# Where the transposing matmuls stand in a block, the place of the x loads, and how much the accumulating DMA adds

## The chip, the cores and the metric

The kernel runs on one core of one Trainium2 chip. The metric is the device time of one execution in microseconds; below it is the median of three runs. The profiled execution is a separate one, with its own time and its own span (first to last instruction).

## The reference, cut to what matters

A dynamic convolution is followed by a two-matmul block with a tanh shrink:

```
w     = softmax(weight_gen over its 7 taps)             # per token and head
conv  = sum over k of w[.., h, k] * x_pad[s + k, h, :]   # 8 heads of 24 channels
h     = conv @ w_in                                      # 192 -> 2048
out   = (h - tanh(h)) @ w_out                            # 2048 -> 192
```

There are 8 x 4096 = 32768 tokens of 192 channels.

## The kernel before, in words

**Tiling.** The tokens are cut into 32 blocks (`NTOT`) of 1024 tokens. Token p*8+j of a block lies in partition p, slot j. Taps are multiplied with the token on the partitions. The result must then be transposed, so that channels lie on the partitions for the first matmul. The 192 channels form three chunks (c = 0, 1, 2) of 64.

**Taps (`products`, L200).** For most blocks GpSimd multiplies all seven taps into three bf16 tiles: `even` (taps 0, 2, 4), `odd` (taps 1, 3, 5) and `last` (tap 6). After tap 5 an accumulating DMA on GpSimd's queue adds `odd` to `even` (L235), but only over the first `ACC` elements of a row. `ACC` is 3*8*192 - 8*64 = 4096 of 4608, so what lies beyond is chunk 2 of the third pair. Blocks 0 to 3 (`PLAIN`) don't use that DMA. The first multiplication of block n+2 is held until `gt1` of block n is done (`behind=last_sub[0]`).

**Transpose and sum (`conv_sums`, L251; `conv_out`).** TensorE multiplies each piece of 64 partitions and 128 columns by an identity, accumulating in PSUM. One chunk of one tap tile takes 8 such matmuls (4 column pieces, two partition halves). There are 4 groups (three of `even`, `last`), and chunk 2 has a fifth, `odd`'s third pair. That makes 8*(4+4+5) = 104 matmuls a block. ScalarE then copies the sums to `convT` (L292): chunk 2 as 128x512, chunks 0 and 1 together as 128x1024.

**First matmul (`gemm1`, L309).** Each of the 16 f tiles (128 of the 2048 inner features) takes 6 matmuls of 512 columns, two row halves side by side, into a PSUM tile `ph`. ScalarE writes `th` = tanh(`ph`) (L320) and VectorE writes `gt` = `ph` - `th` (L321). A `ph` tile is free for reuse only after its `gt`. `ph` and the transposes' `pc` share a rotation of three PSUM tiles (`psum_h`, `bufs=3`), so each new tile waits for the third one before it.

**Second matmul (`gemm2`, L344).** Call number i computes half of token slot i and the other half of slot i-1, alternating, in 16 steps f of two matmuls of 192 columns. There are two PSUM banks, `obank[i % 2]`. After call i, ScalarE copies slot i-1 to `out_sb` (L363). Call i+1 starts slot i+1 in that same bank, so its first matmul waits for that copy. The second matmul is one block behind the first: beside `gemm1` of block n stands `gemm2` of block n-1.

**Order.** The order is written by hand, and each engine keeps it. In block n, six or seven pairs (two `gemm1` tiles, then one `gemm2` call) come first, p = 0, 1, ... VectorE gets small softmax pieces between them: a sum at p = 1, 2, 3 (L155) and a reciprocal at p = 4, 5 (L164). The tail follows: `gemm1` 12 and 13; call 6 with the transposes of chunk 2 mixed in between its steps f = 5 to 12 and their copy after step 12; the transposes of chunks 0 and 1 in one run of 64, and their copy; two steps of call 7; the softmax's normalisation (`softmax_norm`, two VectorE instructions that use chunk 2's `pc` tile as scratch); `gemm1` 14; steps 2 to 8 of call 7; `gemm1` 15; and the rest of call 7. In blocks 1, 2 and 3 (`LATE`) the x load of block n+3 comes at the very end.

**SyncE's queue.** In a block outside `LATE` it holds the x load of block n+3 (L111), then, where a sequence begins, the six halo rows of zeros (L121), the weights of block n+4 (L97), and the output store of block n-2 (L367).

Of the kernel before, what the change touches and what calls it, by code (L numbers as in the profile page):

```python
# [16 lines left out]
def kernel(  # L17
# [10 lines left out]
    B, S, D = x.shape  # L28
    H, K = weight_gen.shape[2], weight_gen.shape[3]
# [3 lines left out]
    R = P // 2  # L33
    HALO = K - 1

    J = 8
    TOK = P * J
    JH = J // 2
    HT = TOK // 2
    NSB = S // TOK  # L40
    NTOT = B * NSB
    NFT = F // P
    NC = D // R
    GC = G // NC
    NPAIR = K // 2
    ACC = NPAIR * J * D - J * R
    PLAIN = (0, 1, 2, 3)
    assert S % TOK == 0 and D % R == 0 and H * GC == R and F % P == 0
    assert NFT == 2 * J, "one token block of the second matmul per pair of f tiles"
# [25 lines left out]
    prods_of = {}  # L75
# [27 lines left out]
    def load_x(n, behind=None):  # L103
        b, s = divmod(n, NSB)
        s0 = s * TOK

        x_t = xpool.tile([P, HALO + J, D], FP32, name="x_t")

        def rows(p0, p1, r0=0, r1=HALO + J):
            first = x[0, 0:1]  # L110
            return nc.sync.dma_start(  # L111
                out=x_t[p0:p1, r0:r1, :],
                in_=bass.AP(
                    tensor=first.tensor,
                    offset=first.offset + (b * S + s0 + p0 * J - HALO + r0) * D,
                    ap=[[J * D, p1 - p0], [D, r1 - r0], [1, D]],
                ),
            )

        def no_halo():  # L120
            nc.sync.dma_start(  # L121
                out=x_t[0:1, 0:HALO, :],
                in_=zero[:].rearrange("o (h d) -> o h d", h=1).to_broadcast([1, HALO, D]),
            )


        if n == 0:
            rows(0, P, HALO, HALO + J)
            rows(16, P, 0, HALO)
            rows(1, 16, 0, HALO)  # L130
            no_halo()
        else:
            dma = rows(0, P)
            if behind is not None:
                order(dma, behind, "order of the loads")
            if s == 0:

                no_halo()
        x_of[n] = x_t
# [11 lines left out]
    def softmax_sum(n, j0=0, j1=J):  # L151

        if j0 == 0:
            zsum_of[n] = wgpool.tile([P, J * H], FP32, name="zsum")
        nc.vector.reduce_sum(  # L155
            out=zsum_of[n][:, j0 * H : j1 * H],
            in_=e_of[n][:, j0:j1].rearrange("p j h k -> p (j h) k"),
            axis=AX.X,
        )
# [40 lines left out]
    def products(n, taps=None, sums=None, hooks={}, behind=None):  # L200

        x_t = x_of.pop(n)
        wsm, wsm_v, e_t, zr = wsm_of.pop(n)
        if e_t is not None:
            scale(nc.gpsimd, wsm[:], e_t, zr[:])
        in_pairs = n not in PLAIN

        even = ppool.tile([P, NPAIR, NC, J, H, GC], BF16, name="even")
        odd = ppool.tile([P, NPAIR, NC, J, H, GC], BF16, name="odd")
        last = ppool.tile([P, NC, J, H, GC], BF16, name="last")  # L210
        dst = {}
        for i in range(NPAIR):
            dst[2 * i] = even[:, i]
            dst[2 * i + 1] = odd[:, i]
        dst[K - 1] = last[:]
        if -1 in hooks:
            hooks[-1]()
        for eng, k, j0, j1 in taps or [(nc.gpsimd, k, 0, J) for k in range(K)]:
            w = wsm_v if eng is nc.vector else wsm[:]
            mul = eng.tensor_mul(  # L220
                dst[k][:, :, j0:j1].rearrange("p c j h g -> p j h c g"),
                x_t[:, k + j0 : k + j1, :].rearrange("p j (h c g) -> p j h c g", h=H, c=NC),
                w[:, j0:j1, :, k : k + 1]
                .rearrange("p j h (k o) -> p j h k o", o=1)
                .to_broadcast([P, j1 - j0, H, NC, GC]),
            )
            if k == 0 and behind is not None:


                order(mul, behind, "pace")  # L230
            if j1 == 1:
                first_halo[0] = mul
            if k == K - 2 and in_pairs:

                nc.gpsimd.dma_start(  # L235
                    out=even[:].rearrange("p i c j h g -> p (i c j h g)")[:, 0:ACC],
                    in_=odd[:].rearrange("p i c j h g -> p (i c j h g)")[:, 0:ACC],
                    accum_op=mybir.AluOpType.add,
                    max_dma_last_dim=4096,
                )  # L240
            if k in hooks:
                hooks[k]()
        if in_pairs:
            groups = [even[:, i] for i in range(NPAIR)] + [last[:]]
            prods_of[n] = [
                groups + ([odd[:, NPAIR - 1]] if c == NC - 1 else []) for c in range(NC)
            ]
        else:
            prods_of[n] = [[dst[k] for k in (sums or range(K))]] * NC

# [47 lines left out]
    def conv(n, *parts):  # L298
        pcs = []
        for _ in conv_sums(n, parts, pcs):  # L300
            pass
        conv_out(n, parts, pcs)

    def gemm1(n, f):
        convT = conv_of[n]
        ph = psum_h.tile([P, 2, HT], FP32, name="ph", tag="ph")
        for c in range(NC):
            for r in range(2):
                nc.tensor.matmul(  # L309
                    ph[:, r, :],  # L310
                    lhsT=w_in[r * R : (r + 1) * R, c, f * P : (f + 1) * P],
                    rhs=convT[r * R : (r + 1) * R, c, :],
                    start=(c == 0),
                    stop=(c == NC - 1),
                )
        th = tpool.tile([P, TOK], FP32, name="th")
        ph_f = ph[:].rearrange("p r t -> p (r t)")
        g1_act[0] = last_act.get(0)
        gt = gpool.tile([P, TOK], BF16, name=f"gt{f}", tag=f"gt{f}")
        last_act[0] = nc.scalar.activation(out=th[:], in_=ph_f, func=ACT.Tanh)  # L320
        last_sub[0] = nc.vector.tensor_sub(gt[:], ph_f, th[:])  # L321
        g_of.setdefault(n, []).append(gt)

    LAST = (NTOT - 1) * J
    LATE = (1, 2, 3)
    LEAD = 5
    FILL, HALF = 2, 9
    half = {}
    out_of = {}

# [139 lines left out]
    def some(sums, m):  # L470
        for _ in range(m):
            next(sums, None)

    load_wg(3)
    load_wg(4)
    for n in range(NTOT):
        if n + 3 < NTOT and n not in LATE:
            load_x(n + 3)
        for p in range(J):
            gemm1(n, 2 * p)  # L480
            gemm1(n, 2 * p + 1)
            if n == 0:


                if p == 3:
                    pcs = []
                    sums = conv_sums(1, ((0, 1),), pcs, obank)
                if 3 <= p <= 6:
                    some(sums, (3 if p == 3 else 1) * 4 * JH)
                if p == 7:  # L490
                    some(sums, K * 4 * JH)
                    conv_out(1, ((0, 1),), pcs)
                    conv(1, (2,))
                continue
            if p == 0 and n == 1:
                softmax_exp(3)
            if p == 1 and n == 1:
                softmax_norm_ramp(3)
                products(3)
            if n + 3 < NTOT:  # L500

                if p == 0:
                    softmax_exp(n + 3)
                if p == 0 and n + 4 < NTOT:
                    load_wg(n + 4)
                if 1 <= p <= 3:
                    softmax_sum(n + 3, (p - 1) * 3, min(p * 3, J))
                if 4 <= p <= 5:
                    softmax_recip(n + 3, (p - 4) * JH, (p - 3) * JH)
            if p < 6 or n == NTOT - 1:  # L510
                gemm2((n - 1) * J + p)
            if p == 0 and 1 < n < NTOT - 2:
                products(n + 2, behind=last_sub[0])
            if p == 6 and n < NTOT - 1:
                break
        if not 1 <= n < NTOT - 1:
            continue


        pcs = []  # L520
        sums = conv_sums(n + 1, ((2,),), pcs)
        mix = len(prods_of[n + 1][2]) * 2 * JH // J

        def between(f):
            if LEAD <= f:
                some(sums, mix)
            if f == LEAD + J - 1:
                conv_out(n + 1, ((2,),), pcs)

        gemm2((n - 1) * J + 6, between=between)  # L530
        conv(n + 1, (0, 1))
        gemm2((n - 1) * J + 7, 0, FILL)
        if n + 3 < NTOT:

            softmax_norm(n + 3, pcs[0][:, 0])
        gemm1(n, NFT - 2)
        gemm2((n - 1) * J + 7, FILL, HALF)
        gemm1(n, NFT - 1)
        gemm2((n - 1) * J + 7, HALF, NFT)
        if n in LATE:  # L540


            load_x(n + 3, last_conv[0])
    gemm2(LAST)
    for j in range(J):
        gemm2_last(j)
# [30 lines left out]
```

The softmax here doesn't subtract the row's maximum and nothing guards it: scores larger than these inputs give would overflow.

## Time and profile before

| | before |
|---|---|
| median of three runs | 762.88 us (762.48 to 765.41) |
| profiled execution: device time / span | 762.46 us / 760.7 us |
| TensorE granted clock | 1.0 over the whole span |
| busy: TensorE / VectorE / ScalarE / GpSimd | 97% / 89% / 84% / 88% |
| `gt`, VectorE, x512 | 603.1 us, 1220 ns each |
| `th`, ScalarE, x512 | 500.5 us, 1022 ns each |
| second matmul, x7936 | 402.6 us, 243 ns each (overlapping) |
| first matmul, x3072 | 391.3 us, 378 ns each (overlapping) |
| tap products on GpSimd, `even` and `odd` / `last` | 2.96 / 3.31 us each |
| accumulating DMA, x28 | 1205 ns of GpSimd each, 8.8 us to landing |
| copy to `convT`, 128x512 / 128x1024 | 598 / 1023 ns |
| copy to `out_sb` | 329 ns |

Busy time of matmuls overlaps, because they are pipelined and their ends are modelled, so where an instruction starts says more than how long it lasted. The middle of the run is a steady state: from the first `gemm1` of one block to that of the next it takes 22.6 us.

### The profile page before, as it was taken

To read this page: it belongs to the slowest core of one execution; us is meant where nothing else is said; L and a number is where in the kernel's file an instruction comes from. 1 tells how busy PE (TensorE), PEld (TensorE's weight loads), DVE (VectorE), ACT (ScalarE), POOL (GpSimd) and SP (SyncE) were. 2 spreads that over 40 slices of the span, in tenths; PEclk is the share of its full clock that TensorE was granted. 3 is DMA by queue.
4 is the path that set the end of the run, shared out by engine and by line. 5 is a ranking of instruction groups with operands and counts; after the bars stand their busy time and mean duration, and the time that the engine had idled before them with its cause. 6 is when DMAs were issued, how large, how long until landed. Compare 5 with 4: busy or idle time off the path is not lost.

```text
span 760.7 us, 32533 instructions
## 1 busy us (share of the span) xinstructions
PE 737.8 (97%) x14848; PEld 575.5 (76%) x14848; DVE 676.3 (89%) x737; ACT 642.3 (84%) x869; POOL 668.7 (88%) x262
## 2 busy tenths in 40 slices
PE   3799999999999999999999999999999999999997
PEld 2477777777778777777877777877777777777777
DVE  7988898989999999999999999998999999998893
ACT  4888888888888888888888888888888888888882
POOL 8999999999999999999999999999999999999000
PEclk9999999999999999999999999999999999999999
DMA  8903347576555775545775655666555577552212
GB/s 216 234 24 129 135 123 186 146 193 146 124 155 157 184 184 130 132 143 149 184 185 130 150 134 149 174 183 171 124 125 151 167 183 180 111 128 62 76 43 85
DMA packets 25399, 110.04 MB, mean 145 GB/s; under 512 B 4671, under 2 KB 9519, under 8 KB 21294
## 3 DMA queue, kind: packets, MB, share of 16 engines
q1 hardware_dynamic: 14718, 77.03, 28.5%
q0 software_dynamic: 10544, 30.94, 25.6%
q8 instruction: 116, 1.90, 1.0%
q14 instruction: 21, 0.17, 0.1%
HBM read 54.52 MB, written 25.17 MB: 105 GB/s over the span
## 4 chain that ended last, share of the span: by engine, by line
PE 93%; DVE 4%; DMA 1%; ACT 1%; issue 1%; ACTq 0%; DVEq 0%
PE obank L344 43%; PE ph L309 43%; PE pc L268 6%; DVE gt L321 3%; PE po L379 1%; DMA x_t<-in_x_dram 1%; DVE odd L220 0%; DMA wg_t<-in_weight_gen_dram 0%; DVE even L220 0%; ACT th L320 0%; DVE zsum L155 0%; ACT e_t L144 0%; DVE zr L164 0%; DVE wsm L194 0%; ACT convT L286 0%
## 5 line engine op out<-in xcount | busy, mean ns | idle before, releaser
L321 DVE TENSOR_TENSOR gt<-ph,th 128x1024 bf16<-128x1024 f32 x512 | 603.1, 1220 | 65.1 <-ACT th L320 61.3
L320 ACT ACTIVATE th<-ph 128x1024 f32<-128x1024 f32 x512 | 500.5, 1022 | 63.0 <-PE ph L309 57.9
L344 PE MATMUL obank<-w_out,gt 64*128 64x192 bf16 x7936 | 402.6, 243 | 1.9 <-issue 0.9
L309 PE MATMUL ph<-convT,w_in 64*128 64x512 bf16 x3072 | 391.3, 378 | 5.0 <-DVE gt L321 2.7
L344 PEld LDWEIGHTS <-gt 64*128 64x128 bf16 x7936 | 350.0, 94 | 59.6 <-issue 1.1
L220 POOL TENSOR_TENSOR even<-x_t,wsm 128x1536 bf16<-128x1536 f32 x93 | 275.2, 2959 | 22.6 <-DVE gt L321 22.4
L220 POOL TENSOR_TENSOR odd<-x_t,wsm 128x1536 bf16<-128x1536 f32 x93 | 275.0, 2957 | 0.0
L309 PEld LDWEIGHTS <-w_in 64*128 64x128 bf16 x3072 | 172.8, 94 | 107.2 <-issue 19.4
L220 POOL TENSOR_TENSOR last<-x_t,wsm 128x1536 bf16<-128x1536 f32 x32 | 105.9, 3308 | 0.0
L363 ACT ACTIVATE out_sb<-obank 128x192 f32<-128x192 f32 x248 | 81.7, 329 | 7.4 <-PE obank L344 3.1
L292 ACT ACTIVATE convT<-pc 128x512 bf16<-128x512 f32 (+1 forms) x63 | 50.7, 807 | 28.4 <-PE pc L268 28.4
L268 PE MATMUL pc<-ident,even 64*128 64x64 bf16 x2256 | 57.2, 191 | 1.2 <-issue 0.9
L268 PEld LDWEIGHTS <-even 64*128 64x128 bf16 x2304 | 54.2, 96 | 2.2 <-issue 1.3
L235 POOL DMA_DIRECT2D even<-odd x28 | 33.7, 1205 | 8.7 <-POOL odd L220 8.7
L268 PE MATMUL pc<-ident,last 64*128 64x64 bf16 x752 | 27.4, 191 | 9.3 <-POOL last L220 9.3
L155 DVE TENSOR_REDUCE zsum<-e_t 128x24 f32<-128x168 f32 (+2 forms) x88 | 27.5, 312 | 3.0 <-ACT e_t L144 3.0
L268 PEld LDWEIGHTS <-last 64*128 64x128 bf16 x768 | 20.2, 96 | 9.6 <-POOL last L220 9.3
L144 ACT ACTIVATE e_t<-wg_t 128x448 f32<-128x448 f32 x32 | 18.4, 578 | 7.3 <-DMA wg_t<-in_weight_gen_dram 7.3
L164 DVE RECIPROCAL zr<-zsum 128x32 f32<-128x32 f32 (+1 forms) x58 | 20.3, 350 | 0.1
L268 PE MATMUL pc<-ident,odd 64*128 64x64 bf16 x464 | 18.8, 197 | 1.7 <-POOL odd L220 0.7
L194 DVE TENSOR_TENSOR wsm<-e_t,pc 128x448 f32<-128x448 f32 x28 | 17.4, 622 | 2.9
L268 PEld LDWEIGHTS <-odd 64*128 64x128 bf16 x512 | 15.4, 99 | 2.5 <-POOL odd L220 0.9
(27 smaller groups left out, 64.3 us busy)
## 6 DMA issues: line engine op xcount, KB each, us to landing
x_t<-in_x_dram SPq DMA_DIRECT2D x31, 1344.0 KB, 9.4
even<-odd POOLq DMA_DIRECT2D x28, 1024.0 KB, 8.8
out_dram<-out_sb SPq DMA_DIRECT2D x31, 768.0 KB, 10.0
wg_t<-in_weight_gen_dram SPq DMA_DIRECT2D x32, 224.0 KB, 6.4
x_t<-in_x_dram SPq DMA_DIRECT2D x1, 768.0 KB
w_out<-in_moe_w_out_dram POOLq DMA_DIRECT2D x1, 768.0 KB, 9.2
out_dram<-out_sb SPq DMA_DIRECT2D x4, 192.0 KB, 1.8
x_t<-in_x_dram SPq DMA_DIRECT2D x1, 504.0 KB
```

Of the source, the lines that this page charges most:

```text
L144: last_exp[0] = nc.scalar.activation(out=e_t[:].rearrange("p j h k -> p (j h k)"), in_=wg_t[:].rearrange("p j h k -> p (j h k)"), func=ACT ...
L155: nc.vector.reduce_sum(out=zsum_of[n][:, j0 * H : j1 * H], in_=e_of[n][:, j0:j1].rearrange("p j h k -> p (j h) k"), axis=AX.X,)
L164: nc.vector.reciprocal(zr_of[n][:, j0 * H : j1 * H], zsum_of[n][:, j0 * H : j1 * H])
L220: mul = eng.tensor_mul(dst[k][:, :, j0:j1].rearrange("p c j h g -> p j h c g"), x_t[:, k + j0 : k + j1, :].rearrange("p j (h c g) -> p j h ...
L235: nc.gpsimd.dma_start(out=even[:].rearrange("p i c j h g -> p (i c j h g)")[:, 0:ACC], in_=odd[:].rearrange("p i c j h g -> p (i c j h g)" ...
L268: nc.tensor.matmul(pc[r][:, col : col + R] if home else pc[:, r, col : col + R], lhsT=prods[c][gi][r * R : (r + 1) * R, c, 2 * j : 2 * j + ...
L292: last_conv[0] = nc.scalar.activation(out=out, in_=pc[:, :, 0:cols].rearrange("p r (cj t) -> p r cj t", t=R), func=ACT.Copy,)
L309: nc.tensor.matmul(ph[:, r, :], lhsT=w_in[r * R : (r + 1) * R, c, f * P : (f + 1) * P], rhs=convT[r * R : (r + 1) * R, c, :], start=(c == ...
L320: last_act[0] = nc.scalar.activation(out=th[:], in_=ph_f, func=ACT.Tanh)
L321: last_sub[0] = nc.vector.tensor_sub(gt[:], ph_f, th[:])
L344: mm = nc.tensor.matmul(po[:, 0:D], lhsT=g_of[n][f][r * R : (r + 1) * R, col : col + P], rhs=w_out[r * R : (r + 1) * R, f, :], start=(r == ...
L363: last_act[0] = nc.scalar.activation(out=out_sb[:, j, :], in_=po[:, 0:D], func=ACT.Copy)
```

## The change

Three things change.

1. The accumulating DMA covers all 4608 elements of a row, as 3 pieces of 1536, and chunk 2 loses its fifth group.
2. In blocks 4 to 30 the tail is laid out anew. Five plain pairs come first. Then `gemm1` 10 and 11, and call 5 with chunk 2 mixed in; the normalisation; `gemm1` 12; steps 0 to 5 of call 6; `gemm1` 13; steps 6 to 15 of call 6 with chunks 0 and 1 mixed in from step 6 to step 13 and their copy after step 13; `gemm1` 14; two steps of call 7; `gemm1` 15; the rest of call 7. The softmax sums become two pieces (p = 1, 2) and the reciprocals move to p = 3, 4.
3. The x load of those blocks is issued after the first call of `gemm2`, and so behind the weights' load and the output store on SyncE's queue.

Blocks 1 to 3 keep the old tail, and block 0 is only rewritten.

```diff
                 nc.gpsimd.dma_start(
-                    out=even[:].rearrange("p i c j h g -> p (i c j h g)")[:, 0:ACC],
-                    in_=odd[:].rearrange("p i c j h g -> p (i c j h g)")[:, 0:ACC],
+                    out=even[:].rearrange("p i c j h g -> p i (c j h g)"),
+                    in_=odd[:].rearrange("p i c j h g -> p i (c j h g)"),
                     accum_op=mybir.AluOpType.add,
...
-            groups = [even[:, i] for i in range(NPAIR)] + [last[:]]
-            prods_of[n] = [
-                groups + ([odd[:, NPAIR - 1]] if c == NC - 1 else []) for c in range(NC)
-            ]
+            prods_of[n] = [[even[:, i] for i in range(NPAIR)] + [last[:]]] * NC
...
+    def conv_between(n, chunks, lead):
+        pcs = []
+        sums = conv_sums(n, (chunks,), pcs)
+        mix = -(-len(prods_of[n][chunks[-1]]) * len(chunks) * 2 * JH // J)
+        def between(f):
+            if lead <= f:
+                some(sums, mix)
+            if f == lead + J - 1:
+                some(sums, K * 4 * JH)
+                conv_out(n, (chunks,), pcs)
+        return between, pcs
...
+            if more and p == (6 if n in LATE else 5):
+                break
...
-                if 1 <= p <= 3:
-                    softmax_sum(n + 3, (p - 1) * 3, min(p * 3, J))
-                if 4 <= p <= 5:
-                    softmax_recip(n + 3, (p - 4) * JH, (p - 3) * JH)
...
+                if 1 <= p <= 2:
+                    softmax_sum(n + 3, (p - 1) * JH, p * JH)
+                if 3 <= p <= 4:
+                    softmax_recip(n + 3, (p - 3) * JH, (p - 2) * JH)
+            out_block(n, p)
             if p == 0 and 1 < n < NTOT - 2:
                 products(n + 2, behind=last_sub[0])
+            if p == 0 and n + 3 < NTOT and n not in LATE:
+                load_x(n + 3)
...
-        gemm2((n - 1) * J + 6, between=between)
-        conv(n + 1, (0, 1))
-        gemm2((n - 1) * J + 7, 0, FILL)
-        if n + 3 < NTOT:
-            softmax_norm(n + 3, pcs[0][:, 0])
-        gemm1(n, NFT - 2)
-        gemm2((n - 1) * J + 7, FILL, HALF)
-        gemm1(n, NFT - 1)
-        gemm2((n - 1) * J + 7, HALF, NFT)
...
+        else:
+            gemm1(n, 10)
+            gemm1(n, 11)
+            between, pcs = conv_between(n + 1, (2,), 5)
+            out_block(n, 5, between=between)
+            norm(n + 3, pcs[0])
+            gemm1(n, 12)
+            out_block(n, 6, 0, 6)
+            gemm1(n, 13)
+            between, _ = conv_between(n + 1, (0, 1), 6)
+            out_block(n, 6, 6, between=between)
+            gemm1(n, 14)
+            out_block(n, 7, 0, 2)
+            gemm1(n, 15)
+            out_block(n, 7, 2)
```

`out_block(n, p, f0, f1, between)` is `gemm2((n - 1) * J + p, f0, f1, between)`.

More of the change, by code (lines that the diff above doesn't have):

```diff
@@ L45 @@
     NPAIR = K // 2
-    ACC = NPAIR * J * D - J * R
     PLAIN = (0, 1, 2, 3)
@@ L325 @@
     LATE = (1, 2, 3)
-    LEAD = 5
-    FILL, HALF = 2, 9
     half = {}
@@ L475, with out_block, norm @@
     load_wg(4)
-    for n in range(NTOT):
-        if n + 3 < NTOT and n not in LATE:
-            load_x(n + 3)
+    load_x(3)
+    for p in range(J):
+        gemm1(0, 2 * p)
+        gemm1(0, 2 * p + 1)
+        if p == 3:
+            pcs = []
+            sums = conv_sums(1, ((0, 1),), pcs, obank)
+        if 3 <= p <= 6:
+            some(sums, (3 if p == 3 else 1) * 4 * JH)
+    some(sums, K * 4 * JH)
+    conv_out(1, ((0, 1),), pcs)
+    conv(1, (2,))
+    def out_block(n, p, f0=0, f1=NFT, between=lambda f: None):
+        gemm2((n - 1) * J + p, f0, f1, between)
+    def conv_between(n, chunks, lead):
+        pcs = []
+        sums = conv_sums(n, (chunks,), pcs)
[4 more added lines that the diff above has]
+            if f == lead + J - 1:
+                some(sums, K * 4 * JH)
+                conv_out(n, (chunks,), pcs)
+        return between, pcs
+    def norm(n, pc):
+        if n < NTOT:
+            softmax_norm(n, pc[:, 0])
+    for n in range(1, NTOT):
         for p in range(J):
+            more = n < NTOT - 1
+            if more and p == (6 if n in LATE else 5):
+                break
             gemm1(n, 2 * p)
             gemm1(n, 2 * p + 1)
[L482 to L494, printed above, removed]
             if p == 0 and n == 1:
@@ L505 @@
                     load_wg(n + 4)
-                if 1 <= p <= 3:
-                    softmax_sum(n + 3, (p - 1) * 3, min(p * 3, J))
-                if 4 <= p <= 5:
-                    softmax_recip(n + 3, (p - 4) * JH, (p - 3) * JH)
-            if p < 6 or n == NTOT - 1:
-                gemm2((n - 1) * J + p)
+                if 1 <= p <= 2:
+                    softmax_sum(n + 3, (p - 1) * JH, p * JH)
+                if 3 <= p <= 4:
+                    softmax_recip(n + 3, (p - 3) * JH, (p - 2) * JH)
@@ L512 @@
+            out_block(n, p)
             if p == 0 and 1 < n < NTOT - 2:
                 products(n + 2, behind=last_sub[0])
-            if p == 6 and n < NTOT - 1:
-                break
-        if not 1 <= n < NTOT - 1:
+            if p == 0 and n + 3 < NTOT and n not in LATE:
+                load_x(n + 3)
+        if not more:
             continue
[L520 to L528, printed above, removed]
@@ L530 @@
-        gemm2((n - 1) * J + 6, between=between)
-        conv(n + 1, (0, 1))
-        gemm2((n - 1) * J + 7, 0, FILL)
-        if n + 3 < NTOT:
-            softmax_norm(n + 3, pcs[0][:, 0])
-        gemm1(n, NFT - 2)
-        gemm2((n - 1) * J + 7, FILL, HALF)
-        gemm1(n, NFT - 1)
-        gemm2((n - 1) * J + 7, HALF, NFT)
-        if n in LATE:
-            load_x(n + 3, last_conv[0])
+        if n in LATE:
+            gemm1(n, 12)
+            gemm1(n, 13)
+            between, pcs = conv_between(n + 1, (2,), 5)
+            out_block(n, 6, between=between)
+            conv(n + 1, (0, 1))
+            out_block(n, 7, 0, 2)
+            norm(n + 3, pcs[0])
+            gemm1(n, 14)
+            out_block(n, 7, 2, 9)
+            gemm1(n, 15)
+            out_block(n, 7, 9)
+            load_x(n + 3, last_conv[0])
+        else:
+            gemm1(n, 10)
+            gemm1(n, 11)
+            between, pcs = conv_between(n + 1, (2,), 5)
+            out_block(n, 5, between=between)
+            norm(n + 3, pcs[0])
+            gemm1(n, 12)
+            out_block(n, 6, 0, 6)
+            gemm1(n, 13)
+            between, _ = conv_between(n + 1, (0, 1), 6)
+            out_block(n, 6, 6, between=between)
+            gemm1(n, 14)
+            out_block(n, 7, 0, 2)
+            gemm1(n, 15)
+            out_block(n, 7, 2)
```

## The prediction

> **What bounds the kernel now.** I read the page's busy shares first, then the chain that ended last, then one steady block of the timeline.
>
> ```profile
> PE 737.8 (97%) x14848; PEld 575.5 (76%) x14848; DVE 676.3 (89%) x737; ACT 642.3 (84%) x869; POOL 668.7 (88%) x262
> ...
> PE 93%; DVE 4%; DMA 1%; ACT 1%; issue 1%; ACTq 0%; DVEq 0%
> PE obank L344 43%; PE ph L309 43%; PE pc L268 6%; DVE gt L321 3%; PE po L379 1%; DMA x_t<-in_x_dram 1%; DVE odd L220 0%; DMA wg_t<-in_weight_gen_dram 0%; DVE even L220 0%; ACT th L320 0%; DVE zsum L155 0%; ACT e_t L144 0%; DVE zr L164 0%; DVE wsm L194 0%; ACT convT L286 0%
> ```
>
> TensorE sets the time. The chain in order of time, over one block (start, length, engine, line, count), shows how full it is:
>
> ```profile
> 402.32 0.93 PE pc L268 x64
> 403.25 0.17 PE obank L344 x4
> 403.42 0.68 PE ph L309 x6
> 404.10 0.58 PE obank L344 x14
> 404.68 0.65 PE ph L309 x6
> 405.32 0.58 PE obank L344 x14
> 405.90 1.47 PE ph L309 x12
> 407.37 1.32 PE obank L344 x32
> 408.69 1.29 PE ph L309 x12
> ...
> 428.54 1.47 PE ph L309 x12
> ```
>
> A block takes 428.54 - 405.90 = 22.64 us. A pair of first-matmul tiles takes 1.29, a second-matmul call 1.32, 64 transposes 0.93. These give 0.647 per tile, 0.0825 per step of a call and 0.0145 per transpose. A block's own instructions are 8 x (1.295 + 1.32) + 104 x 0.0145 = 22.43. So only 0.2 us of a block is waiting, and most of it shows: the first pair takes 1.47 instead of 1.29. The timeline says why:
>
> ```profile
> 402.11 0.60 ACT L292 ACTIVATE convT<-pc 128x512 bf16<-128x512 f32 x1 [0.36 <-PE pc L268]
> 402.61 0.33 ACT L363 ACTIVATE out_sb<-obank 128x192 f32<-128x192 f32 x1
> 403.29 1.02 ACT L292 ACTIVATE convT<-pc 128x1024 bf16<-128x1024 f32 x1 [0.36 <-PE pc L268]
> 404.21 2.17 ACT L320 ACTIVATE th<-ph 128x1024 f32<-128x1024 f32 x2
> 405.26 4.74 DVE L321 TENSOR_TENSOR gt<-ph,th 128x1024 bf16<-128x1024 f32 x4 [1.18 <-ACT th L320]
> 406.54 0.33 PEld L309 LDWEIGHTS <-w_in 64*128 64x128 bf16 x5 [0.29 <-issue]
> ```
>
> `gt14` starts at 405.26; tile 1 of the next block, which reuses its PSUM tile, starts at 406.54 instead of 405.72 + 0.65 = 406.37, so 0.17 us is lost. From these rows I take the latencies that I step with:
>
> - PE end to ScalarE start 0.21 (0.22 for a `convT`).
> - Start to start on ScalarE: 0.92 after a `th` or large `convT`, 0.50 after a small one.
> - `th` start to `gt` start 1.06.
> - `gt` to `gt` 1.137 (4.74 for four, less the last one's 1.22, is 3.52; two take 2.36).
> - `gt` start to reuse of its tile by TensorE 1.28.
>
> Stepped so, the block before comes to 22.65, with waits of 0.18 (tile 1), 0.04 (tile 14) and 0.01: the steps reproduce the trace.
>
> **What the Trainium skill says.** "TensorE: Matmul & The Clock Gate", section "Wait — 56ns, not 53.3ns?", gives N / 2.4 GHz + about 2.5 ns per matmul. For 64, 192 and 512 columns that is 29, 82.5 and 216 ns, and with two row halves side by side the trace agrees (0.93/32 = 29, 1.32/16 = 82.5, 1.295/6 = 216). So the transposes have no hidden price. The same page's "Specifications" lists ScalarE and VectorE as strict FIFO. On TensorE, it adds, only weight loads are pulled ahead. The trace agrees for ScalarE: `out_sb` at 402.61 stands between the two `convT` as written. "DMA: Bandwidth & Descriptors", section "SDMA does more than copy", caps an accumulating piece at 2048 elements. No row shows it, but as compiled the DMA is 128 x 2 x 2048 before and 128 x 3 x 1536 after.
>
> **The change, part by part.**
>
> *Eight transposes fewer:* 8 x 0.0145 = 0.116 us of TensorE a block, in 28 blocks (4 to 31).
>
> *The larger DMA:* 1152 KB instead of 1024, 3 pieces a row instead of 2. It now takes 8.8 us to land (up to 10.1). By bytes that becomes 9.9, by pieces 13.2; I keep both. Before, it is issued 0.78 us ahead of a block's start (404.94 against 405.72). The products start 4.35 after it and are issued 17.5 later, so in a 23.3 us block at 1.5 ahead. It lands 8.4 to 11.7 into the block. Chunk 2's transposes come at 5 x 2.615 + 1.295 + 0.495 = 14.9 (17.5 before), so at least 3 us remain. On GpSimd the issue occupies 0.78 us of the queue (404.94 to 405.72). The w_out load, with 16 runs a row, took 1.23 us there against this DMA's 1.20, so a third piece costs 0 to 0.4; I take 0.1. GpSimd waits 1.00 us a block for `gt`, which covers it.
>
> *The x loads (25 of them):* SyncE waited 440.9 us for GpSimd's `last` at this load, with the weights' load and the store queued behind. Afterwards these two go first (0.4 to 1.3 and 0.4 to 1.0 us of issue) and the load follows `out_sb`, ready at 409.21 here. It starts 1 to 2 us later than its 409.11, lands 9.4 us on, and is due only at the next block's products, 4.35 + 22.6 after this block's start: 12 us to spare. If late, GpSimd would be late next, then the DMA, then the transposes. Cost 0. The halo rows no longer hold the store back; nothing waits for that either.
>
> *Softmax pieces:* 32-column sums instead of 24, 24, 16. From 317 and 259 ns for 168 and 112 elements, 224 take 376. A pair leaves VectorE 2.615 - 2 x 1.137 = 0.34, so each of two pairs runs 0.04 behind, and the reciprocals (0.343) don't catch up. A tile reused an odd place on has about 0.06 to spare, so 0.01 shows; 0 to 0.05.
>
> *The new tail (27 blocks).* Counted from the start of tile 10:
>
> 1. `gt10` starts at 0.647 + 0.21 + 1.06 = 1.92, VectorE's lag makes it 1.99, so its PSUM tile is free at 3.27. TensorE is through tiles 10, 11, call 5 and 32 transposes at 1.295 + 1.32 + 0.465 = 3.08. Tile 12, three places on, **waits 0.19**. Before, the two `pc` tiles and 0.93 us of transposes stood between.
> 2. Chunk 2's last transpose ends at 2.83, its `convT` starts at 3.05, `out_sb` behind it at 3.55, done 3.88, seen by TensorE (0.06, as for `gt`) at 3.94. Call 6 needs that bank, after tile 12, at 3.91: **0.03**.
> 3. After six steps, tile 13 and one step TensorE stands at 5.17. Chunks 0 and 1 need chunk 2's `pc`, free after the normalisation: 1.99 + 2 x 1.137 + 0.32 + 0.62 + 0.06 = 5.26. **0.09**.
> 4. Step 13, the last with transposes, ends at 5.26 + 0.93 + 7 x 0.0825 = 6.76 (T). The large `convT` starts at T + 0.22, and `out_sb` is written behind it: start T + 1.14, done T + 1.47, seen T + 1.53. Call 7's first matmul needs that bank and stands, behind two steps and tile 14, at T + 0.165 + 0.647 = T + 0.81. **It waits 0.72.** Before, call 6 ended ahead of the 0.93 us run, so `out_sb` was copied ahead of the large `convT`. Behind the waiting matmul stand tile 15 and the next block's first pair, and so both other engines.
> 5. That wait lets `gt14` catch up, so tile 1's 0.18 and tile 14's 0.04 go.
>
> Sum per block: -0.12 + 0.19 + 0.03 + 0.09 + 0.72 - 0.18 - 0.05 + 0.01 = **+0.69**. Over 27 blocks 18.6. The two without softmax lose 0.1 less each; block 3's saved 0.12 goes into a wait for `gt12` (its run of 64 reaches the PSUM tile earlier). So +18.5. The profiled execution, 762.46 (span 760.7 and 1.8 around it), would take 781.0. The median lies 0.4 above it: **781.4 us**. Blocks become 23.3 us.
>
> **Rivals.**
>
> *A, only the bank wait or smaller slot waits.* If items 1 to 3 are hidden, a block gains 0.72 - 0.12 - 0.23 = 0.37: 773 us. Without the bank wait but with the others, stepping gives 22.98 (tile 1 then waits 0.35): +0.33, 772. For it: items 2 and 3 are under 0.1.
>
> *B, more.* VectorE's lag grows to 0.2 over the pairs and the copies take 0.1 longer: +0.95, 788. For it: VectorE is within 0.34 us a pair of full.
>
> *C, the other side: TensorE stays bound by its own instructions.* If `out_sb` were free by T + 0.81 and tile 12 covered, the block is 22.43 - 0.12 = 22.31, 0.33 less: 754 us. It decides if all waits together stay below 0.32 us. Against it: the large `convT` alone holds ScalarE 0.92 us, more than the 0.81 that TensorE has.
>
> *D, the accumulating DMA becomes the bound.* From a landing above 16 us on, chunk 2 is late; at 20 us every block takes 3.6 longer, 860 us. Against it: 13.2 is the upper estimate.
>
> **How the numbers follow.** Forecast 0.70, A 0.12, B 0.09, C 0.05, D 0.04. Under 0.5% (3.8 us) either way can't be told from no change; of C's 0.05, 0.02 goes to a case that stops there. So faster 0.03, same 0.02, slower 0.95. The range reaches to A and B: 772 to 789.
>
> **What would show it.** Blocks of 23.3 us; second matmuls waiting about 0.7 us for `out_sb` once a block, that copy starting 0.92 after the large `convT`; the first pair at 1.29 again; 224 transposes fewer; landing of the DMA 9 to 13 us with no wait on it. I am wrong if `out_sb` is copied ahead of `convT`, if blocks take 22.3 us, or if transposes wait for a DMA.

## The result

The changed kernel takes **782.47 us** (median of four runs, 780.31 to 785.24). The kernel before takes 763.99 us (four runs, 762.48 to 765.41). The ratio is 1.0244, with a 95% interval of 1.0201 to 1.0287: 18.5 us slower, where the prediction said 781.4 us and 18.5 us slower. The profiled execution is the longest of the four, at 785.24 us with a span of 783.5 us.

The page's busy shares and the chain that ended last, after the change:

```profile
PE 741.6 (95%) x14624; PEld 570.2 (73%) x14624; DVE 676.0 (86%) x709; ACT 645.6 (82%) x869; POOL 671.3 (86%) x262
...
PE 78%; POOL 8%; DMA 4%; issue 4%; DVE 3%; ACT 2%; SPq 0%; ACTq 0%; DVEq 0%; POOLq 0%
...
L338 PE MATMUL obank<-w_out,gt 64*128 64x192 bf16 x7936 | 425.6, 243 | 15.2 <-ACT out_sb L357 14.6
...
even<-odd POOLq DMA_DIRECT2D x28, 1152.0 KB, 9.9
```

TensorE has 224 matmuls fewer, as expected, and every engine's share of the span has fallen: none became the bound in its place. What is new is the third line: the second matmuls (L344 before, L338 now) sit idle 15.2 us, nearly all of it ahead of them released by the output copy on ScalarE. Before, they sat idle 1.9 us.

The end of one steady block in the chain in order of time (start, length, what), in the new tail; "issue" is time in which the profile shows nothing that was waited for:

```profile
417.19 0.19 ACT convT L288
417.38 0.63 issue
...
418.11 0.33 ACT out_sb L357
...
418.48 0.34 PE obank L338 x4
...
420.63 1.29 PE ph L305 x12
```

Two things are to be seen. The chain leaves TensorE between 417.19 and 418.48 and runs over ScalarE's two copies. And the first pair of the next block (420.63) takes 1.29 us again, not 1.47: the old wait of tile 1 is gone. ScalarE's timeline of the same block shows the order that causes it:

```profile
413.32 0.60 ACT L288 ACTIVATE convT<-pc 128x512 bf16<-128x512 f32 x1 [0.25 <-PE pc L264]
413.81 0.33 ACT L357 ACTIVATE out_sb<-obank 128x192 f32<-128x192 f32 x1
...
417.19 1.02 ACT L288 ACTIVATE convT<-pc 128x1024 bf16<-128x1024 f32 x1 [0.62 <-PE pc L264]
418.11 0.33 ACT L357 ACTIVATE out_sb<-obank 128x192 f32<-128x192 f32 x1
```

TensorE's timeline of the same block has where call 5, tile 12, call 6, the transposes of chunks 0 and 1, tile 14 and call 7 start:

```profile
411.56 0.68 PE L338 MATMUL obank<-w_out,gt 64*128 64x192 bf16 x12
...
413.46 0.82 PE L305 MATMUL ph<-convT,w_in 64*128 64x512 bf16 x6
414.19 0.67 PE L338 MATMUL obank<-w_out,gt 64*128 64x192 bf16 x12
...
415.46 0.29 PE L264 MATMUL pc<-ident,even 64*128 64x64 bf16 x8
...
417.15 0.81 PE L305 MATMUL ph<-convT,w_in 64*128 64x512 bf16 x6
418.48 0.34 PE L338 MATMUL obank<-w_out,gt 64*128 64x192 bf16 x4 [0.53 <-ACT out_sb L357]
```

The output copy starts 0.92 us after the large `convT`, and call 7's first matmul follows it at 418.48. Tile 14 started at 417.15 and takes 0.65, so it was over at 417.80, and TensorE waited 0.68 us for the bank. (The profile counts 0.53, because the modelled end of a matmul lies later.)

A block now takes 23.25 us (from one large `convT` to the next, in nearly every steady block), where before it took 22.64.

### The profile page after: what moved, and what is told of

It reads as the page before. It is cut to its first block, busy times and chain, and to the rows that moved or that the text cites. A ratio compares the mean times of both kernels' runs of the same rounds, so it can differ in the third digit from the quotient of the medians.

```text
span 783.5 us, 32057 instructions
## 1 busy us (share of the span) xinstructions
PE 741.6 (95%) x14624; PEld 570.2 (73%) x14624; DVE 676.0 (86%) x709; ACT 645.6 (82%) x869; POOL 671.3 (86%) x262
## 4 chain that ended last, share of the span: by engine, by line
PE 78%; POOL 8%; DMA 4%; issue 4%; DVE 3%; ACT 2%; SPq 0%; ACTq 0%; DVEq 0%; POOLq 0%
PE obank L338 37%; PE ph L305 35%; PE pc L264 5%; POOL even L219 3%; POOL odd L219 3%; DVE gt L317 2%; DMA even<-odd 2%; PE po L373 1%; ACT out_sb L357 1%; DMA x_t<-in_x_dram 1%; DMA x_t<-zero 1%; POOL last L219 1%; ACT convT L288 1%; ACT th L316 0%; DVE odd L219 0%
## 5 line engine op out<-in xcount | busy, mean ns | idle before, releaser
L338 PE MATMUL obank<-w_out,gt 64*128 64x192 bf16 x7936 | 425.6, 243 | 15.2 <-ACT out_sb L357 14.6
L338 PEld LDWEIGHTS <-gt 64*128 64x128 bf16 x7936 | 354.1, 94 | 83.4 <-issue 27.6
L264 PE MATMUL pc<-ident,even 64*128 64x64 bf16 x2256 | 70.3, 191 | 4.7 <-DMA even<-odd 3.8
L264 PEld LDWEIGHTS <-even 64*128 64x128 bf16 x2304 | 65.5, 96 | 11.8 <-DVE wsm L193 5.3
L234 POOL DMA_DIRECT2D even<-odd x28 | 36.1, 1289 | 8.6 <-POOL odd L219 8.6
L264 PEld LDWEIGHTS <-last 64*128 64x128 bf16 x768 | 24.1, 96 | 10.0 <-POOL last L219 9.8
L154 DVE TENSOR_REDUCE zsum<-e_t 128x32 f32<-128x224 f32 (+1 forms) x60 | 23.5, 391 | 2.8 <-ACT e_t L143 2.8
L143 ACT ACTIVATE e_t<-wg_t 128x448 f32<-128x448 f32 x32 | 18.4, 578 | 8.8 <-DMA wg_t<-in_weight_gen_dram 8.8
L373 PE MATMUL po<-w_out,gt 64*128 64x192 bf16 x256 | 11.0, 243 | 0.0
L373 PEld LDWEIGHTS <-gt 64*128 64x128 bf16 x256 | 10.8, 93 | 0.0
```

The costliest lines, as they stand in the source:

```text
L154: nc.vector.reduce_sum(out=zsum_of[n][:, j0 * H : j1 * H], in_=e_of[n][:, j0:j1].rearrange("p j h k -> p (j h) k"), axis=AX.X,)
L234: nc.gpsimd.dma_start(out=even[:].rearrange("p i c j h g -> p i (c j h g)"), in_=odd[:].rearrange("p i c j h g -> p i (c j h g)"), accum_o ...
L264: nc.tensor.matmul(pc[r][:, col : col + R] if home else pc[:, r, col : col + R], lhsT=prods[c][gi][r * R : (r + 1) * R, c, 2 * j : 2 * j + ...
L338: mm = nc.tensor.matmul(po[:, 0:D], lhsT=g_of[n][f][r * R : (r + 1) * R, col : col + P], rhs=w_out[r * R : (r + 1) * R, f, :], start=(r == ...
L373: nc.tensor.matmul(po[:, r, 0:D], lhsT=g_of[n][f][r * R : (r + 1) * R, col : col + P], rhs=w_out[r * R : (r + 1) * R, f, :], start=(f == 0 ...
```

## The experiments

Each kernel differs from the kernel before, or from the changed one, only by the edit shown or described. "Steady block" is the time from one large `convT` to the next in the profiled run. Blocks 4, 5 and 6 are irregular: there GpSimd is still behind, and their times are given apart, each as the interval that ends with the large `convT` that stands in that block's tail. (Two of the expectations below count otherwise: their "blocks 4 and 5" with two long times are blocks 4 and 6 here.)

### The accumulating DMA alone, in the kernel before

```diff
-                    out=even[:].rearrange("p i c j h g -> p (i c j h g)")[:, 0:ACC],
-                    in_=odd[:].rearrange("p i c j h g -> p (i c j h g)")[:, 0:ACC],
+                    out=even[:].rearrange("p i c j h g -> p i (c j h g)"),
+                    in_=odd[:].rearrange("p i c j h g -> p i (c j h g)"),
...
-            groups = [even[:, i] for i in range(NPAIR)] + [last[:]]
-            prods_of[n] = [
-                groups + ([odd[:, NPAIR - 1]] if c == NC - 1 else []) for c in range(NC)
-            ]
+            prods_of[n] = [[even[:, i] for i in range(NPAIR)] + [last[:]]] * NC
```

> The kernel before with the full accumulating DMA and 8 transposes fewer a block, its tail, softmax pieces and x loads as they were. Theory 1 (the three rotating PSUM tiles set the tail): the 0.12 us saved a block comes back as a wait of the run of 64 transposes for the gt of tile 12; blocks stay at 22.60 to 22.65 us and the time within 1 us of before. Theory 2 (TensorE is bound by its own instructions): blocks shrink to 22.52 us and the time falls by 3 us. The DMA lands in 9 to 13 us and nobody waits for it in the steady state under either.

Measured: 765.4 us against 764.49 (ratio 1.0015, interval 1.0004 to 1.0026). The steady block is 22.63 us. Its chain in order of time:

```profile
404.80 0.25 PE obank L341 x6
405.05 1.05 PE pc L265 x64
...
408.74 1.46 PE ph L306 x12
```

The run of 64 transposes takes 1.05 us instead of 0.93: the 0.12 us that eight transposes fewer saved stand there as a wait. The timelines show for what. The run needs the PSUM tile of tile 12, and the `gt` that frees it starts at 403.71 and takes 1.22, until 404.93; the first transpose starts at 404.99, 0.06 later. In the kernel before the same three times are 400.86, 402.08 and 402.14, but there call 6 kept TensorE until 402.14, so nothing was lost. Theory 1 holds. In this tail eight transposes less work for the bounding engine are worth nothing, because the next PSUM tile of the rotation is not free any earlier. The steady blocks give none of the 0.9 us on the total; in the profiled runs blocks 4 and 6 took 24.93 and 23.82 us here and 23.32 and 23.62 in the kernel before.

### The new tail alone

The changed kernel with the old accumulating DMA and its fifth group, and with the x loads at the start of a block.

> The changed kernel with the old accumulating DMA (two pieces, chunk 2 keeps its fifth group) and the x loads at their old place: only the new tail and the softmax pieces remain. Theory (the wait of call 7 for the output copy is the cost): blocks of 23.25 to 23.36 us, call 7 waits 0.6 to 0.7 us, time 17 to 19 us above before, as the whole change. Rival (the larger DMA or the later x loads carry a good part): blocks under 23.0 us and less than 10 us above before.

Measured: 781.38 us, ratio 1.022 (1.02 to 1.024), 16.9 us above before; the steady block is 23.32 us, and the second matmuls waited for the output copy in every block (0.52 us as the profile counts idle time). The tail, with its softmax pieces, carries nearly the whole loss, and no transposes waited for a DMA here. (27 x 0.68 would be 18.4 us. The runs of the kernel before, beside which this one was timed, spread from 761.14 to 766.64 us, so sums over blocks of one profiled run meet the medians to a microsecond or two, not to tenths.) With its eight transposes more than the changed kernel it is only 0.07 us a block longer, not 0.12: part of them fills waiting time here too.

### The x loads alone, in the kernel before, twice

```diff
-        if n + 3 < NTOT and n not in LATE:
+        if n == 0:
             load_x(n + 3)
...
                 products(n + 2, behind=last_sub[0])
+            if p == 0 and n > 0 and n + 3 < NTOT and n not in LATE:
+                load_x(n + 3)
```

> The kernel before with only the x loads of blocks 4 to 28 moved behind the first call of the second matmul. Theory: steady blocks stay at 22.64 us, time within 1 us of before. Rival (the early blocks of the changed kernel, where the accumulating DMA took up to 15 us to land, were late because of the moved load and store): about 2 to 3 us appear between block 4 and block 7 and nothing after.

> The kernel before with only the x loads moved, once more, because its gain of 0.3% is near what a measurement can tell. If it is real: 1.5 to 2.5 us under before with an interval below 1, steady blocks 22.64 us and blocks 4 and 5 at 22.64 too, where before has 23.3 and 23.6. If it was chance: ratio 1.000 within 0.2%.

Measured: 762.41 us against 764.49 (0.9971, 0.9959 to 0.9983), and again 761.94 against 764.51 (0.9969, 0.9958 to 0.998). The steady block is 22.64 us both times. The gain of 0.3% is real. The first expectation missed it ("within 1 us"), and its rival, that the moved load costs the early blocks time, has fallen the other way. Blocks 4 and 6 took 23.32 and 23.62 us before; here they took 22.64 and 22.63, in the second run 22.79 and 22.91. So 1.7 and 1.2 us of the gain of 2.1 and 2.6 are seen there; the kernel before stood at two places in these blocks (0.50 and 0.91 us), for a reason that the next section shows. So this third of the change is a small gain, and **this version is faster than both kernels**; it beats the kernel before by 0.3%.

### The x loads put back, in the changed kernel

```diff
     for n in range(1, NTOT):
+        if n + 3 < NTOT and n not in LATE:
+            load_x(n + 3)
...
-            if p == 0 and n + 3 < NTOT and n not in LATE:
-                load_x(n + 3)
```

> The changed kernel with only its x loads put back to the start of a block. Theory: steady blocks 23.25 us as in the changed kernel. If the moved load and store made the early accumulating DMA late, the waits for it (3.8 us of GpSimd, 3.8 us of TensorE before block 6) are gone and the time is 2 to 4 us below the changed kernel; if they come from the larger DMA alone, they stay.

Measured: 784.72 us, ratio 1.0266 (1.0244 to 1.0287); steady block 23.25 us. The total did not fall, so the second half of that expectation is a miss. Of the DMA waits TensorE's fell from 3.8 us to 0.4 us and GpSimd's stayed (3.5), but another wait took their place. TensorE's timeline of block 4, here:

```profile
128.38 0.23 PE L264 MATMUL pc<-ident,even 64*128 64x64 bf16 x4 [0.43 <-DMA even<-odd]
136.04 0.23 PE L264 MATMUL pc<-ident,even 64*128 64x64 bf16 x4 [3.27 <-issue]
```

and the same stretch and the next block in the changed kernel:

```profile
130.22 0.23 PE L264 MATMUL pc<-ident,even 64*128 64x64 bf16 x4 [1.52 <-DMA even<-odd]
134.85 0.23 PE L264 MATMUL pc<-ident,even 64*128 64x64 bf16 x4 [0.25 <-issue]
...
156.30 0.23 PE L264 MATMUL pc<-ident,even 64*128 64x64 bf16 x4 [2.27 <-DMA even<-odd]
```

In the changed kernel the transposes of chunk 2 stood 1.52 and 2.27 us for the accumulating DMA. With the loads put back, the transposes in the same block stood 3.27 us for nothing that the profile shows ("issue"). Waits of that kind appear also in block 4 of other kernels, with and without the change.

The traces tell what they are. Each page has a DMA queue named "instruction", here that of the kernel before and of the changed one (packets, MB, share of 16 engines):

```profile
q8 instruction: 116, 1.90, 1.0%
...
q8 instruction: 114, 1.87, 0.9%
```

TensorE has 14848 matmuls and 14848 weight loads before, 14624 of each after: one packet of 16 KB for every 256 of its instructions. Count TensorE's instructions in order of their start. From 60 us on, the ten traces have 33 waits of TensorE of more than 0.06 us that the profile calls "issue". All 33 stand ahead of the instruction 193 or 195 behind a multiple of 256, and all end 2.3 to 3.3 us after the start of one packet of this queue, 1.0 to 1.6 us after its end. In block 4 it is the same instruction, number 4545, in every kernel:

| kernel | wait | packet starts | TensorE goes on | between |
|---|---|---|---|---|
| before | 0.50 us | 127.21 | 129.67 | 2.46 us |
| DMA alone | 2.12 us | 130.20 | 132.58 | 2.38 us |
| new tail alone | 1.94 us | 129.39 | 131.80 | 2.41 us |
| x loads put back | 3.27 us | 133.69 | 136.04 | 2.35 us |
| changed | 0.25 us | 132.51 | 134.85 | 2.34 us |

So TensorE waits for its own instructions, which are fetched late. Why the packet is late is not shown; with the loads put back, it starts 0.9 us after TensorE has stopped (132.77), at the end of a stretch in which the DMA engines were at least 60% busy (132 to 134 us). In these profiles the place of the x loads changes such waits in blocks 4 to 6: 0.50 and 0.91 us in the kernel before, none above 0.2 us in the two with the loads moved.

### The x loads and the accumulating DMA, without the new tail

The kernel before with two of the edits above together: that of the accumulating DMA and that of the x loads.

> The kernel before with the x loads moved and the full accumulating DMA (8 transposes fewer), old tail. Theory: steady blocks stay at 22.63 us. For blocks 4 and 5 two views: if the store and load that come first delay the accumulating DMA, moving the x loads cures these blocks here too and the time is that of the x loads alone, 762 to 763 us; if it is the size of the DMA (as the 24.9 and 23.8 us of these blocks with the larger DMA alone suggest), they keep 1 to 3 us of it and the time is 764 to 766 us.

Measured: 763.02 us against 764.51 (0.9982, 0.9966 to 0.9997), steady block 22.63 us. Block 4 took 24.81 us and block 6 23.07, where the DMA alone had 24.93 and 23.82 and the x loads alone 22.64 and 22.63. The total lies at the edge of the first view, 0.6 to 1.1 us above the x loads alone. Moving the x loads leaves block 4 nearly as it is (0.49 us waiting for the DMA, 1.44 us for instructions) and takes 0.75 us from block 6, so neither view holds whole.

### The output copy ahead of the large convT, in the changed kernel

```diff
-            between, _ = conv_between(n + 1, (0, 1), 6)
+            between, pcs = conv_between(n + 1, (0, 1), 6, copy=False)
             out_block(n, 6, 6, between=between)
+            conv_out(n + 1, ((0, 1),), pcs)
```

(`copy=False` leaves out the copy after step 13.)

> The changed kernel with one edit: the large convT copy is written behind the output copy of call 6 instead of ahead of it. Theory (call 7 waits for its PSUM bank because the output copy stands behind the large convT): that wait, 0.6 to 0.7 us, is gone; but tanh 14 now starts later behind convT, so tile 1 of the next block waits 0.4 to 0.5 us for the gt of tile 14, and blocks go from 23.25 to about 23.1 (22.95 to 23.15), 3 to 8 us less. Rival (the wait is for something else, the transposes or TensorE's own restart): blocks stay at 23.25.

Measured: 776.14 us, 6.3 us below the changed kernel (ratio to before 1.0157, 1.0117 to 1.0198); steady block 22.98 us. ScalarE's and TensorE's timelines, here:

```profile
411.60 0.33 ACT L357 ACTIVATE out_sb<-obank 128x192 f32<-128x192 f32 x1 [0.79 <-PE obank L338]
411.83 1.02 ACT L288 ACTIVATE convT<-pc 128x1024 bf16<-128x1024 f32 x1
412.73 1.95 ACT L316 ACTIVATE th<-ph 128x1024 f32<-128x1024 f32 x2
```

```profile
411.39 0.81 PE L305 MATMUL ph<-convT,w_in 64*128 64x512 bf16 x6
412.04 0.33 PE L338 MATMUL obank<-w_out,gt 64*128 64x192 bf16 x4
...
414.01 0.81 PE L305 MATMUL ph<-convT,w_in 64*128 64x512 bf16 x6
415.07 0.82 PE L305 MATMUL ph<-convT,w_in 64*128 64x512 bf16 x6 [0.25 <-DVE gt L317]
```

Call 7 starts 0.65 us after tile 14, so the bank wait of 0.68 is gone, by nothing but the order of two copies. In its place tile 1 starts 1.06 us after tile 0 instead of 0.65: it waits 0.41 us for `gt14`, whose tanh now stands behind the large `convT`. Both were expected at that size. The cause of the largest term is shown. In this order it is traded against a smaller wait.

### Tiles 14 and 15 ahead of call 7, in the changed kernel

```diff
             gemm1(n, 14)
-            out_block(n, 7, 0, 2)
             gemm1(n, 15)
-            out_block(n, 7, 2)
+            out_block(n, 7)
```

> The changed kernel with one edit: tiles 14 and 15 both go ahead of call 7, so that its first matmul comes 0.8 us later and its bank is free by then; nothing is taken away. Theory: the bank wait falls to under 0.1 us, tile 1 waits 0.2 to 0.3 us, blocks 22.9 to 23.0 us, so 7 to 10 us below the changed kernel and still 7 to 10 us above before, because the waits for tile 12 and for the transposes' tile stay. Rival (without the bank wait the new tail beats the old one): blocks under 22.64 us.

Measured: 771.01 us, ratio to before 1.0091 (1.0056 to 1.0126); steady block 22.82 us, slightly better than expected. The chain in order of time has the pair 14 and 15 at 1.39 us and the next block's first pair at 1.46 us, against 1.295: waits of 0.10 and 0.17, and none for the bank. The rival falls: without the bank wait the new tail is still 0.18 us a block longer than the old one. That is 27 x 0.18 = 4.9 us of the 6.6 us that this kernel lies above before; the profiled runs show more than the rest in its blocks 4 and 5 (25.58 and 26.57 us).

## Why the prediction was right, point by point

**The bank wait (item 4, 0.72 us).** Measured 0.68. Its mechanism is shown by the reordered copies, its size by the changed kernel's timeline. It rests on ScalarE keeping the written order, which the trace shows here too: `out_sb` starts at 418.11, 0.92 us after the large `convT`. (The row on strict order that the prediction cites from the Trainium skill's "TensorE: Matmul & The Clock Gate" stands in the table at the head of that page, under no heading of its own.)

**The other waits of the new tail (items 1 to 3).** From TensorE's starts in one steady block: call 5 begins at 411.56, so it and its 32 transposes are over at 411.56 + 1.32 + 0.465 = 413.345, and tile 12 starts at 413.46, **0.12** later (predicted 0.19). Tile 12 ends at 414.11 and call 6 starts at 414.19, **0.08** later (0.03). The transposes of chunks 0 and 1 stand **0.05** (0.09), which the profile lists as a wait for `wsm`, the normalisation. VectorE's lag, put at 0.07, was not there: `gt10` starts at 412.19, 1.92 us after tile 10 (410.27), where 1.99 was expected. That alone moves the three waits to what was measured.

**The waits that go (item 5).** The first pair is back at 1.29 us, as predicted.

**The sum.** Own instructions 22.31, waits 0.12 + 0.08 + 0.05 + 0.68 = 0.93, together 23.24; measured 23.25. The same sum closes for the other kernels:

| kernel | own instructions | waits seen | sum | measured |
|---|---|---|---|---|
| DMA alone | 22.31 | tile 1 0.17, transposes 0.12, tile 14 0.03 | 22.63 | 22.63 |
| output copy first | 22.31 | 0.12 + 0.08 + 0.05, tile 1 0.41 | 22.97 | 22.98 |
| tiles 14, 15 first | 22.31 | 0.12 + 0.08 + 0.05, tile 15 0.10, tile 1 0.17 | 22.83 | 22.82 |

**Block 3's saved 0.12 us goes into a wait for `gt12`.** The DMA alone shows just that, in every block.

**Where it was off.** The tail is worth 27 x 0.61 = 16.5 us, not 18.6. (The working's own terms, 18.6 less 0.2 for the two blocks without softmax, give 18.4 and not 18.5.) A step that was put at nothing made up for the difference: the larger DMA. That forecast and medians both say 18.5 us is therefore luck in part.

"At least 3 us remain" is true of the steady state, where no transposes waited for the DMA, but not of blocks 4 and 5. There two things were left out. The first is a wait of GpSimd. This is the first `odd` product of block 5, in the kernel before and in the changed one:

```profile
99.37 3.34 POOL L220 TENSOR_TENSOR odd<-x_t,wsm 128x1536 bf16<-128x1536 f32 x1
...
104.87 2.90 POOL L219 TENSOR_TENSOR odd<-x_t,wsm 128x1536 bf16<-128x1536 f32 x1 [3.76 <-DMA even<-odd]
```

In all six kernels with the larger DMA it starts 0.07 us after block 4's DMA has landed, after a wait of 2.3 to 3.8 us. In the four with the smaller one it starts while that DMA is still under way. What in the program sets this wait is not shown; the same edit also takes away the transposes that read `odd`. GpSimd has no slack in these blocks, so block 5's DMA is issued at 119.51, where it is 114.42 in the kernel before and 114.90 with the new tail alone. The new tail asks for its result 2.6 us earlier than the old one, and the transposes stand 1.52 us. The second is the landing: the next DMA took 15.0 us, above my 13.2, and the transposes stand 2.27 us in block 5.

This is rival D, in two blocks instead of in all, and "transposes wait for a DMA" was named as a sign of being wrong. It takes both parts of the change: with the new tail alone no transposes waited for a DMA, with the larger DMA and the old tail they waited 0 and 0.49 us. In the profiled runs blocks 4 to 6 grew from 69.58 to 73.58 us, by 4.0, of which the steady loss explains 3 x 0.61 = 1.8. The 2.2 us that remain are about the 3.8 us of waits for the DMA less the 1.7 us by which blocks 4 and 6 of the kernel before exceed its steady ones. So 16.5 + 2.2 = 18.7 us.

The x loads were put at 0 too, again from a steady block, where that holds. In the kernel before, moving them is worth 2.1 to 2.6 us, of which 1.7 and 1.2 are seen in the early blocks. In the changed kernel putting them back cost 2.3 us by the medians, but its interval overlaps that of the changed kernel.

The profiled execution shows 22.8 us more span, not 18.5. The first 3.7 us of this arise before the large `convT` in block 1's tail (64.30 us against 60.59), and the other 19.1 are close to the 18.7 above. VectorE waited 2.2 us in that first stretch for an x load. But for two softmax pieces of block 1 the instructions there are the same. The other profiled kernels with this start reach that point between 61.17 and 63.58 us, those with the old start between 60.59 and 61.40. Most of the 3.7 us is thus the spread of the start; whether about a microsecond of it belongs to the change is open.

**The rivals.** A asked for 0.33 to 0.37 us a block more and B for 0.95; measured is 0.61. A's second case, the bank wait gone and the other waits kept, is the kernel with the output copy ahead: stepped 22.98 us, measured 22.98. C did not occur: no tail here came near 22.31 us.

## What to carry to other kernels

When a full engine still waits a little, ask what releases each wait before counting on work taken away: here three PSUM tiles rotate, each is held for about 3.2 us by matmul, tanh and subtraction, and in the old tail eight transposes fewer only let TensorE arrive earlier at the same release. A buffer's release stands in the queue of the engine that frees it: here a small copy written behind a large one started 0.92 us after it, and TensorE lost 0.68 us of that. Step a new order through one block with the durations of the old trace, and then once more for the first blocks, where an engine that is later ahead may still be behind.

## What the runs showed of the hardware that was not expected

- The accumulating DMA grew from 1024 to 1152 KB and from 2 to 3 pieces a row. Its landing rose from 8.8 to 9.9 us, in proportion to the bytes (1.125) and not to the pieces (1.5); GpSimd's time for it rose from 1.20 to 1.29 us.
- With the x loads moved, its longest landing was 14.0 to 15.0 us in four kernels (15.0 in block 5 of the changed kernel, with an output store and an x load issued within 4.3 us behind it); with the x loads at their old place it was at most 11.7 us (two kernels).
- TensorE stood 0.25 to 3.3 us in block 4 for its own instructions, of which one 16 KB packet brings 256. It went on 2.3 to 2.5 us after the packet's start. The profile shows this only as "issue".
